# Laying the weight pieces of a gated last layer beside other chunks of an expert layer (attention, experts, SwiGLU on one core)

## The chip, the cores and the metric

The kernel runs on one core of one Trainium2 chip. A core has TensorE (PE in the rows; its weight loads are PEld), VectorE (DVE), ScalarE (ACT), GpSimd (POOL) and SyncE (SP, which here only issues DMA transfers). Each engine takes its own instructions in the order of the program and waits on semaphores for the others. The metric is the device time of one execution in microseconds (us), the median of the runs.

## The reference

Three layers follow each other, all in float32, on 4 x 576 = 2304 tokens of width 512:

```
attn = softmax(scale * q k^T + mask) v          # 8 heads of 64; 4 local (32 keys), 4 strided (every 32nd)
x    = attn, heads side by side                 # 2304 x 512
e    = argmax(x @ w_gate)                       # one of 8 experts per token
x    = p_e * sigmoid(x @ w_output_gate)_e * (relu(x @ w1[e]) @ w2[e])      # 512 -> 1024 -> 512
xn   = x / sqrt(mean(x*x) + 1e-6) * rms_g
g, v = xn @ w_gate2, xn @ w_val                 # 512 -> 1536, twice
out  = (g * sigmoid(g) * v) @ w_out             # 1536 -> 512
```

## The kernel before, in words

**Precision.** Each float32 operand of a matmul is split into a rounded part (names that end in `hi` or `h`) and the rest (`lo`, `l`), and each product is made of three matmuls: hi x hi, hi x lo, lo x hi.

**Stages.** Attention and routing take the first 130 us. Then come the 8 experts, sorted by their number of tokens: the first, with room for 256 tokens, then the fullest with 384, then 352, 336, 320, 304, 288 and 272. Then comes the last layer in 6 blocks of 384 tokens.

**Experts.** An expert's hidden width of 1024 is cut into 8 chunks of 128, so there are 64 chunks, `ch` 0 to 63; chunks 0 to 7 belong to the first expert, 8 to 15 to the fullest. For a chunk, `up(ch)` makes 12 matmuls into `hps` (L752 to L754), ScalarE writes `hhi` (L757) and VectorE `hlo` (L758); `down(ch)` makes 12 matmuls into four banks `y` (L776 to L778). TensorE's order is up(1), down(0), up(2), down(1) and so on; before chunks 4 and 5 of an expert stand transposes (L721) of the next expert's tokens, which ScalarE and VectorE take out (`xhi` L738, `xlo` L739). A chunk's weights are one transfer of 512 KB (`raw`, L176, four buffers), asked for four chunks ahead and split two chunks ahead into `whi` (ScalarE, L184) and `wlo` (VectorE, L185), three buffers. A `raw` transfer waits until VectorE has split the chunk that had the buffer before. GpSimd gathers the next expert's tokens (`xg`, L194), for the fullest expert three tiles of up to 128 rows of 528 float32 values.

**Pieces of the last layer's first weights.** `w_gate2` and `w_val` come as 24 pieces of 512 KB (float32 words and, of each, the bits that the narrow type takes), two for each of the 12 chunks of the width 1536. `prep_gv` transfers a piece into `gvr` (L653, two buffers), and `narrow` makes `gvh` and `gvl` of it with seven instructions: ScalarE L100 (`n_ab`, reads `gvr`) and L109 (`gvh`), VectorE L102, L105, L106, L108 (on `n_a`) and L110 (`gvl`). L109 waits for L108, L110 for L109. The table `GVC` names the chunks beside which the pieces stand, in order. Only the first VectorE instruction is tied to a place (behind the `wlo` of two chunks on); where the others and the transfer stand in their engines' queues is decided by the scheduler, which goes by times of its own, and so the tables' effect is seen in the order of the built program alone.

**Last layer.** `up2(u)` makes 24 matmuls of 384 columns into two banks `g` (L928 to L930), then follow sg (ScalarE L933, VectorE L934 and L935), `ahi` (ScalarE L938) and `alo` (VectorE L939); `down2(u)` makes 9 matmuls of 512 columns (L952 to L954) behind `up2(u + 1)`. In the first block (u = 0 to 11) the 12 pieces of `w_out` (`wr`, L899) are narrowed as well, by the same `narrow`, into `woh` and `wol`, one for each u, needed by `down2(u)`. Pieces of `GVC` that have no place beside an expert come here too, at u = 0, 2, 4 and so on; they share the two buffers of `wr`. In each block the next block is normalised: sums of squares (ScalarE L665, VectorE L667), `ss` (TensorE L676), `f` (VectorE L678, L679, GpSimd L680, VectorE L681), `fb` (TensorE L688).

```python
            if ch in GVC:
                prep_gv(pr_p, GVC.index(ch), queue_behind(last_split))
...
            if u % 2 == 0 and GV1 + u // 2 < 2 * NFC2:
                prep_gv(wr_p, GV1 + u // 2, queue_behind(last_up))
```

Of the kernel before, what the change touches and what calls it, by code (L numbers as in the profile page):

```python
# [41 lines left out]
BLK = 384  # L42
NBLK = N // BLK
WARM = (1, 2, 4, 2, 2, 1, 1)
GVC = (1, 3, 5, 7, 9, 11, 13, 15, 17, 19, 21, 24, 26, 28, 31, 33, 36, 39, 41, 44, 47, 50, 53, 57)
GV1 = len(GVC)
PB0 = (44, 46, 49, 51, 55, 57, 59, 61)
NB = (1, 3, 4, 5, 7, 8, 9, 10)
# [65 lines left out]
def attention_moe_swiglu(ctx: ExitStack, tc, qkv, va_l, va_s, wgd, cst_p, cst_a, cst_o, w12, wgv, wo, rmsg, out):  # L114
# [521 lines left out]
    def queue_behind(to):  # L636

        return lambda ins: tc.add_manual_dep(
            ins, to.name, mybir.DependencyInfo(mybir.DependencyClass.NoSync, mybir.DependencyReason.DATA),
            reason="order of issue on one engine")  # L640
# [9 lines left out]
    def prep_gv(pool, i, order=None):  # L650
        i, s = divmod(i, 2)
        r = pool.tile([128, KD * 128, 2], U32, tag="wr", name="gvr", bufs=2)
        nc.sync.dma_start(out=r.rearrange("p n w -> p (n w)"), in_=wgv[i, s].bitcast(U32))  # L653
        narrow(nc, pool, r, gvh[i][:, s].rearrange("p k f -> p (k f)"), gvl[i][:, s].rearrange("p k f -> p (k f)"), order)
# [47 lines left out]
    with m1:  # L702
# [7 lines left out]
        def turn_x(r, ks=range(KD)):  # L710
            cap = CAPS[r]
            if r in xT:
                hi, lo = xT[r]
            else:
                hi = xt_p.tile([128, KD, CAP], F32R, tag="xhi", name="xhi")
                lo = xt_p.tile([128, KD, CAP], F32R, tag="xlo", name="xlo")
                xT[r] = (hi, lo)

            def turn(j, k, ps):
                o, n, g = xg_t[r, j]  # L720
                nc.tensor.transpose(out=ps[:, o:o + n], in_=g[0:n, 128 * k:128 * (k + 1)],  # L721
                                    identity=cs("ident", n)[:, 0:n])

            nj = -(-cap // 128)
            if r == 0:

                pss = [ps_y.tile([128, CAP], F32, tag=f"y{k}", name="xp0") for k in range(KD)]
                for j in range(nj):
                    for k in range(KD):
                        turn(j, k, pss[k])  # L730
            for k in ks:
                if r == 0:
                    ps = pss[k]
                else:
                    ps = ps_x.tile([128, CAP], F32, tag="xp", name="xp")
                    for j in range(nj):
                        turn(j, k, ps)
                nc.scalar.copy(out=hi[:, k, 0:cap], in_=ps[:, 0:cap])  # L738
                nc.vector.tensor_tensor(out=lo[:, k, 0:cap], in0=ps[:, 0:cap], in1=hi[:, k, 0:cap].bitcast(F32),  # L739
                                        op=ALU.subtract)  # L740
# [96 lines left out]
        for ch in range(NCH):  # L837
# [11 lines left out]
            if fc in (4, 5) and r + 1 < E:  # L849
                turn_x(r + 1, (0, 1) if fc == 4 else (2, 3))  # L850
            if ch in GVC:
                prep_gv(pr_p, GVC.index(ch), queue_behind(last_split))
            if ch == 4:
# [327 lines left out]
```

## Time and profile before

| | us |
|---|---|
| runs | 853.64, 852.37, 849.71; median 852.37 |
| the profiled execution | 846.85 |
| its span, first to last instruction | 844.9 |
| TensorE busy in it | 825.6 |
| VectorE, ScalarE, GpSimd busy | 487.0, 335.6, 78.2 |

The profile is of one execution, which is 5.5 us shorter than the median of the runs. TensorE's busy time holds each matmul's whole passage through the array; matmuls overlap, so the pace of a row of matmuls is the distance of their starts, not their duration.

### The profile page before, as it was taken

The numbers are of one execution on the slowest core, as the hardware profiler recorded it, in microseconds if no ns is written. First come the engines' busy times: TensorE is split into PE (matmuls) and PEld (weight loads), VectorE is DVE, ScalarE is ACT, GpSimd is POOL, SyncE is SP. The second block draws the span as 40 slices with busy tenths as digits, with TensorE's granted clock in tenths as the row PEclk, the third lists the DMA queues.
The fourth block names the chain that finished last, engine by engine and source line by source line (L and its number), as shares of the span: only waits on it lengthen the run. The fifth ranks groups of instructions, "written<-read, shape, count | busy, mean of one in ns | idle before, by whom it ended". The sixth has DMA issues, their size and how long they took to land.

```text
span 844.9 us, 13837 instructions
## 1 busy us (share of the span) xinstructions
PE 825.6 (98%) x5230; PEld 766.6 (91%) x5230; DVE 487.0 (58%) x1342; ACT 335.6 (40%) x699; POOL 78.2 (9%) x76
## 2 busy tenths in 40 slices
PE   9999997999999999999999999999999999999996
PEld 6998865899999999999999999999999999999995
DVE  3889986978877788868875252234225222422221
ACT  3777644755556556644433131122213111212111
POOL 0000002425321101000001000100000010001001
PEclk9999999999999999999999999999999999999998
DMA  8788217899897697534321010101011010001000
GB/s 331 275 292 294 64 38 250 277 260 218 261 242 217 229 281 247 180 121 138 94 93 38 1 38 1 38 1 38 1 38 38 1 38 1 2 0 38 1 1 38
DMA packets 41765, 100.39 MB, mean 119 GB/s; under 512 B 9440, under 2 KB 23136, under 8 KB 41696
## 3 DMA queue, kind: packets, MB, share of 16 engines
q1 hardware_dynamic: 37840, 89.45, 34.2%
q0 software_dynamic: 3856, 10.05, 3.4%
q8 instruction: 41, 0.67, 0.3%
q14 instruction: 28, 0.23, 0.1%
HBM read 84.73 MB, written 14.75 MB: 118 GB/s over the span
## 4 chain that ended last, share of the span: by engine, by line
PE 73%; issue 15%; DVE 6%; DMA 3%; ACT 1%; POOL 1%; POOLq 0%; SPq 0%
PE g L928 8%; PE g L929 8%; PE g L930 8%; PE hps L752 4%; PE hps L753 4%; PE hps L754 4%; PE y L777 4%; PE y L778 4%; PE y L776 4%; PE o L953 4%; PE o L954 4%; PE o L952 4%; PE ops L349 3%; PE tps L331 2%; PE s L304 2%
## 5 line engine op out<-in xcount | busy, mean ns | idle before, releaser
L934 DVE TENSOR_TENSOR sg<-sg,g 128x384 f32<-128x384 f32 x72 | 39.8, 553 | 150.5 <-ACT sg L933 150.3
L933 ACT ACTIVATE sg<-g 128x384 f32<-128x384 f32 x72 | 35.3, 490 | 176.1 <-PE g L930 175.9
L185 DVE TENSOR_TENSOR wlo<-raw,whi 128x1024 fp32r<-128x1024 f32 (+1 forms) x66 | 78.6, 1192 | 33.6 <-ACT whi L184 29.4
L928 PE MATMUL g<-xn1h,gvh 128*128 128x384 f32 x288 | 97.7, 339 | 0.0
L929 PE MATMUL g<-xn1l,gvh 128*128 128x384 f32 x288 | 97.3, 338 | 0.0
L930 PE MATMUL g<-xn1h,gvl 128*128 128x384 f32 x288 | 97.1, 337 | 0.0
L928 PE MATMUL g<-xn0h,gvh 128*128 128x384 f32 x288 | 96.8, 336 | 0.0
L929 PE MATMUL g<-xn0l,gvh 128*128 128x384 f32 x288 | 96.4, 335 | 0.0
L930 PE MATMUL g<-xn0h,gvl 128*128 128x384 f32 x288 | 96.3, 335 | 0.0
L938 ACT CAST ahi<-sg 128x384 fp32r<-128x384 f32 x72 | 36.8, 512 | 132.1 <-DVE sg L935 132.1
L953 PE MATMUL o<-wol,ahi 128*128 128x512 f32 x216 | 85.4, 396 | 0.0
L954 PE MATMUL o<-woh,alo 128*128 128x512 f32 x216 | 85.2, 394 | 0.0
L952 PE MATMUL o<-woh,ahi 128*128 128x512 f32 x216 | 85.2, 394 | 0.0
L184 ACT CAST whi<-raw 128x1024 fp32r<-128x1024 f32 (+1 forms) x66 | 67.6, 1024 | 43.2 <-PE y L777 39.2
L752 PE MATMUL hps<-xhi,whi 128*128 128x256 f32 (+7 forms) x256 | 80.6, 315 | 0.8 <-ACT xhi L738 0.6
L754 PE MATMUL hps<-xhi,wlo 128*128 128x256 f32 (+7 forms) x256 | 79.4, 310 | 1.4 <-DVE wlo L185 1.4
L777 PE MATMUL y<-hlo,whi 128*128 128x256 f32 (+7 forms) x256 | 78.2, 306 | 2.1 <-DVE hlo L758 2.1
L753 PE MATMUL hps<-xlo,whi 128*128 128x256 f32 (+7 forms) x256 | 78.9, 308 | 0.4 <-DVE xlo L739 0.4
L778 PE MATMUL y<-hhi,wlo 128*128 128x256 f32 (+7 forms) x256 | 78.1, 306 | 0.0
L776 PE MATMUL y<-hhi,whi 128*128 128x256 f32 (+7 forms) x256 | 77.8, 306 | 0.0
L323 ACT ACTIVATE p<-u,nm 96x128 f32<-96x128 f32 (+2 forms) x176 | 60.1, 389 | 41.6 <-DVE nm L314 41.4
L935 DVE TENSOR_TENSOR sg<-sg,g 128x384 f32<-128x384 f32 x72 | 39.9, 554 | 59.1 <-PE g L930 58.7
(176 smaller groups left out, 1658.6 us busy)
## 6 DMA issues: line engine op xcount, KB each, us to landing
raw<-in_w SPq DMA_DIRECT2D x62, 512.0 KB
gvr<-in_wgv SPq DMA_DIRECT2D x24, 512.0 KB
qk<-in_qkv SPq DMA_DIRECT2D x14, 864.0 KB
wr<-in_wo SPq DMA_DIRECT2D x12, 512.0 KB
va<-in_va_l SPq DMA_DIRECT2D x4, 972.0 KB
yb<-yt_dram SPq DMA_DIRECT2D x20, 192.0 KB
va<-in_va_s SPq DMA_DIRECT2D x3, 810.0 KB
x_dram<-xs SPq DMA_DIRECT2D x24, 96.0 KB
```

The source lines that it names most:

```text
L752: mm(out=ps, lhsT=wh[:, w], rhs=xh[:, k, 0:cap], start=(k == 0), stop=False)
L753: mm(out=ps, lhsT=wh[:, w], rhs=xl[:, k, 0:cap], start=False, stop=False)
L754: last = mm(out=ps, lhsT=wl[:, w], rhs=xh[:, k, 0:cap], start=False, stop=(k == KD - 1))
L776: mm(out=ps, lhsT=wh[:, w], rhs=hi, start=(fc == 0), stop=False)
L777: mm(out=ps, lhsT=wh[:, w], rhs=lo, start=False, stop=False)
L778: mm(out=ps, lhsT=wl[:, w], rhs=hi, start=False, stop=(fc == NFC1 - 1))
L928: mm(out=ps, lhsT=wh, rhs=xh[d], start=(d == 0), stop=False)
L929: mm(out=ps, lhsT=wh, rhs=xl[d], start=False, stop=False)
L930: last_mm = mm(out=ps, lhsT=wl, rhs=xh[d], start=False, stop=(d == KD - 1)).ins
L952: mm(out=po[j], lhsT=hi[:, s], rhs=woh[i], start=(i == 0), stop=False)
L953: mm(out=po[j], lhsT=hi[:, s], rhs=wol[i], start=False, stop=False)
L954: mm(out=po[j], lhsT=lo[:, s], rhs=woh[i], start=False, stop=(i == NFC2 - 1))
```

## The change

The table of places is replaced, and nothing else:

```diff
-GVC = (1, 3, 5, 7, 9, 11, 13, 15, 17, 19, 21, 24, 26, 28, 31, 33, 36, 39, 41, 44, 47, 50, 53, 57)
+GVC = (6, 8, 9, 11, 14, 15, 17, 19, 22, 23, 25, 27, 30, 32, 34, 35, 38, 40, 43, 47, 50, 54)
 GV1 = len(GVC)
```

Pieces beside the experts, first to last: 4, 4, 3, 4, 3, 3, 2, 1 before; 1, 5, 4, 3, 4, 3, 2, 0 now. The table has 22 places in place of 24, so the last two pieces (both of the last chunk of the width 1536, read first by `up2(11)`) go to the last layer's first block, to u = 0 and u = 2.

ScalarE, from the end of `up(1)` in the first expert on. `hhi` is a chunk's rectified hidden part (chunks 1, 2, 3 and so on), `whi` a chunk's split weights (chunks 3, 4, 5 and so on), `n_ab<-gvr` the first instruction of a piece. Before:

```order
L757 ACTIVATE hhi<-hps 128x256
L184 CAST whi<-raw 128x1024
L757 ACTIVATE hhi<-hps 128x256
L100 ACTIVATE n_ab<-gvr 128x512
L184 CAST whi<-raw 128x1024
L757 ACTIVATE hhi<-hps 128x256
L184 CAST whi<-raw 128x1024
L109 CAST gvh_2472<-n_a 128x512
L100 ACTIVATE n_ab<-gvr 128x512
```

The same place now:

```order
L757 ACTIVATE hhi<-hps 128x256
L184 CAST whi<-raw 128x1024
L757 ACTIVATE hhi<-hps 128x256
L184 CAST whi<-raw 128x1024
L100 ACTIVATE n_ab<-gvr 128x512
L757 ACTIVATE hhi<-hps 128x256
L184 CAST whi<-raw 128x1024
L757 ACTIVATE hhi<-hps 128x256
L184 CAST whi<-raw 128x1024
L738 CAST xhi<-xp 128x384 x2
```

The piece of chunk 6 begins on ScalarE almost where the piece of chunk 1 began, one instruction later: behind `whi` of chunk 4, ahead of `hhi` of chunk 3. The other pieces' instructions are gone from here.

SyncE, from the transfer of chunk 5's weights on (`raw` of chunks 5, 6, 7 and so on; `gvr` are pieces; L166 and L782 read an expert's number or offset into a register). The difference at this place, before with -, now with +:

```order
@@ -115,44 +115,50 @@
 L176 ISA
 L176 DMA raw<-in_w 128x1024
-L653 DMA gvr<-in_wgv 128x1024
-L176 ISA
-L176 DMA raw<-in_w 128x1024
-L653 DMA gvr<-in_wgv 128x1024
-L176 ISA
-L176 DMA raw<-in_w 128x1024
-L166 TENSOR_LOAD rank_i
-L166 ISA x2
```

and now:

```order
+L176 ISA
+L176 DMA raw<-in_w 128x1024
+L166 TENSOR_LOAD rank_i
+L166 ISA x2
+L653 DMA gvr<-in_wgv 128x1024
+L176 ISA
+L176 DMA raw<-in_w 128x1024
```

The row with the first `gvr` stood behind `raw` of chunk 5 and stands now behind `raw` of chunk 7 and a register read.

TensorE in the first block of the last layer, around the normalisation of the next block: `ss` is the sum over the width, `fb` the factor spread over the partitions. Before, from the second k-step of `up2(5)` to the first matmul of `up2(6)`, in parts:

```order
L928 MATMUL g_5959<-xn0h,gvh_2477 128x384
L676 MATMUL ss<-cst_p_sb,s 128x1 x3
L929 MATMUL g_5959<-xn0l,gvh_2477 128x384
...
L954 MATMUL o_5765<-woh_5628,alo 128x512
L688 MATMUL fb<-cst_p_sb,f 128x128 x3
L928 MATMUL g_6017<-xn0h,gvh_2478 128x384
```

Now, from the thirteenth matmul of `up2(6)` to the first of `down2(5)`:

```order
L928 MATMUL g_6030<-xn0h,gvh_2478 128x384
L676 MATMUL ss<-cst_p_sb,s 128x1 x3
L929 MATMUL g_6030<-xn0l,gvh_2478 128x384
...
L930 MATMUL g_6030<-xn0h,gvl_2490 128x384
L688 MATMUL fb<-cst_p_sb,f 128x128 x3
L952 MATMUL o_5746<-woh_5607,ahi 128x512
```

Both go one u later, and where 20 matmuls of `up2` and 9 of `down2` stood between `ss` and `fb`, 11 of `up2` stand now. On VectorE each of the two pieces stands as a whole ahead of a piece of `w_out`: the first behind `wol` of u = 1, the second behind `wol` of u = 3.

## Rows read from the trace of the kernel before

**Rows 1.** The page's busy times: us, share of the span, instructions.
```profile
PE 825.6 (98%) x5230; PEld 766.6 (91%) x5230; DVE 487.0 (58%) x1342; ACT 335.6 (40%) x699; POOL 78.2 (9%) x76
```
**Rows 2.** Busy time of each engine by stretch: stretch, length, busy, clock, DMA share, GB/s.
```profile
134.30:164.10 29.80, 25.57 (x193) 24.23 (x194) 24.07 (x43) 18.52 (x32) 7.62 (x7) 0.94 0.87 308
164.10:198.00 33.90, 33.90 (x207) 33.82 (x206) 28.63 (x44) 20.17 (x34) 15.39 (x14) 1.00 0.91 239
...
198.00:230.10 32.10, 32.10 (x205) 32.06 (x205) 26.59 (x40) 19.55 (x32) 12.48 (x11) 1.00 0.92 247
...
376.30:410.00 33.70, 33.37 (x183) 31.40 (x182) 27.00 (x49) 15.00 (x29) 1.26 (x1) 1.00 0.43 137
```
**Rows 3.** TensorE in order of time: start, duration, line, tiles.
```profile
143.06 0.28 PE L752 MATMUL hps<-xhi,whi 128*128 128x256 f32 x1
...
145.10 0.28 PE L752 MATMUL hps<-xhi,whi 128*128 128x256 f32 x1
...
164.09 0.33 PE L752 MATMUL hps<-xhi,whi 128*128 128x384 f32 x1
...
164.44 0.34 PE L754 MATMUL hps<-xhi,wlo 128*128 128x384 f32 x1
```
**Rows 4.** TensorE's waits in the first expert, in order of time: [idle <- releaser].
```profile
147.96 0.38 PE L777 MATMUL y<-hlo,whi 128*128 128x256 f32 x1 [1.10 <-DVE hlo L758]
...
150.43 0.39 PE L754 MATMUL hps<-xhi,wlo 128*128 128x256 f32 x1 [0.66 <-DVE wlo L185]
...
160.35 0.38 PE L777 MATMUL y<-hlo,whi 128*128 128x256 f32 x1 [1.04 <-DVE hlo L758]
```
**Rows 5.** ScalarE and VectorE behind those waits, in order of time.
```profile
147.15 0.67 ACT L100 ACTIVATE n_ab<-gvr 128x512 f32<-128x512 f32 x1 [2.82 <-DMA gvr<-in_wgv]
...
147.15 0.43 DVE L102 TENSOR_SCALAR n_a<-gvr 128x512 uint32<-128x512 uint32 x1 [1.91 <-DMA gvr<-in_wgv]
...
155.34 0.39 ACT L757 ACTIVATE hhi<-hps 128x256 fp32r<-128x256 f32 x1 [0.34 <-PE hps L754]
...
159.89 0.41 DVE L758 SCALAR_TENSOR_TENSOR hlo<-hps,hhi 128x256 fp32r<-128x256 f32 x1
```
**Rows 6.** Busy time in the stretch of the third wait, columns as rows 2.
```profile
155.00:163.00 8.00, 6.96 (x60) 6.64 (x59) 8.00 (x17) 4.86 (x10) 3.97 (x3) 1.00 0.80 265
```
**Rows 7.** Busy time of the instructions on `n_a` alone: VectorE, ScalarE, clock, DMA.
```profile
376.30:451.00 74.70, 38.21 (x60) 7.40 (x12) 1.00 0.33 107
```
**Rows 8.** SyncE's issues in the first expert, in order of time.
```profile
140.80 0.34 SPq L653 DMA_DIRECT2D gvr<-in_wgv  x1
142.47 0.33 SPq L176 DMA_DIRECT2D raw<-in_w  x1
...
145.27 5.46 SPq L176 DMA_DIRECT2D raw<-in_w  x2
```
**Rows 9.** Busy time and GB/s while these transfers ran, columns as rows 2.
```profile
145.90:149.30 3.40, 2.30 (x20) 2.09 (x19) 2.12 (x5) 1.89 (x3) 0.28 (x1) 1.00 0.96 360
```
**Rows 10.** VectorE and TensorE in the last layer's first block, in order of time.
```profile
388.63 0.69 DVE L110 TENSOR_TENSOR wol<-n_a,woh 128x512 fp32r<-128x512 f32 x1 [0.15 <-ACT woh L109]
...
392.99 0.69 DVE L110 TENSOR_TENSOR wol<-n_a,woh 128x512 fp32r<-128x512 f32 x1 [0.22 <-ACT woh L109]
...
397.32 0.39 PE L952 MATMUL o<-woh,ahi 128*128 128x512 f32 x1
...
406.87 0.83 PE L676 MATMUL ss<-cst_p_sb,s 128*128 128x1 f32 x6 [0.33 <-DVE s L667]
...
410.04 0.16 DVE L681 TENSOR_TENSOR f<-f,gd 128x3 f32<-128x3 f32 x1 [0.74 <-POOL f L680]
```
**Rows 11.** Busy time and granted clock around the end of routing, columns as rows 2.
```profile
130.00:134.00 4.00, 1.74 (x10) 0.84 (x8) 2.73 (x13) 1.16 (x4) 0.30 (x1) 1.00 0.80 224
134.00:138.00 4.00, 3.33 (x17) 3.13 (x18) 3.51 (x8) 2.66 (x7) 0.00 (x0) 0.70 0.82 263
138.00:139.00 1.00, 1.00 (x6) 1.00 (x6) 0.26 (x1) 0.25 (x1) 0.00 (x0) 0.50 1.01 389
```

## The prediction

> **What bounds the kernel now.** I read the page first: TensorE is busy for 825.6 of 844.9 us [rows 1], so only its idle time and its pace can move the end. The busy times by stretch then say where idle time is: beside the fullest and the third expert TensorE is busy for all of 33.90 and 32.10 us, and beside the first for 25.57 of 29.80, with VectorE at 24.07; the first block of the last layer misses 0.33 us of 33.70 [rows 2]. Moving work off VectorE can therefore gain in the first expert alone, and elsewhere the move can only lose.
>
> For the size I take TensorE's pace from starts: 18 matmuls of 256 columns in 145.10 - 143.06 = 2.04 us, 0.113 each, and 0.175 for 384 columns [rows 3]. Twelve matmuls of the first expert last 1.36 us, so a chunk's 24 take 2.72 us. Three waits break this pace: 1.10 us at 147.96, 0.66 at 150.43 and 1.04 at 160.35 [rows 4]. A wait costs more than its idle time: the matmul ahead of it counts as busy for 0.28 us where the pace is 0.113 (+0.17), and the first one behind it takes about 0.1 longer. So they cost 1.37 + 0.93 + 1.31 = 3.6 us, which bounds the gain. The first 6 us of the expert lie before any piece is asked for [rows 8] and do not change.
>
> What ends these waits: the first two go back to the first piece, which landed at 147.15. VectorE's first instruction of it, ahead of `hlo` of chunk 2, had kept VectorE idle for 1.91 us, and ScalarE's, ahead of the split of chunk 4, ScalarE for 2.82 us [rows 5]. The third is VectorE's own queue: `hhi` of chunk 5 was ready at 155.7, `hlo` began at 159.89 [rows 5], and between 155 and 163 VectorE was busy for 8.00 of 8.00 us [rows 6].
>
> **The change, part by part.**
>
> *A piece's cost.* In the last layer 12 pieces kept VectorE busy for 38.21 us, ScalarE's `gvh` half apart [rows 7]: 3.18 us of VectorE a piece.
>
> *First expert, third wait.* Less 3.18 us for one piece, VectorE's 8.00 us [rows 6] become 4.8, so `hlo` no longer comes late: 1.31 us gained. The one piece left has its VectorE part behind the split of chunk 8, at the expert's end.
>
> *First expert, first two waits.* They do not go, by the order: `n_ab<-gvr` still stands ahead of `hhi` of chunk 3 on ScalarE, and its transfer now stands behind three `raw` transfers, of which the third (chunk 7) was issued at 145.27, when the split of chunk 3 was done [rows 8]. Some 0.35 us for that issue and a register read lie ahead of the piece: I put it at 146.3. When it lands has two bounds. Before, it took 147.15 - 140.80 = 6.35 us [rows 5, 8], which would be 152.65. At the 360 GB/s that the queues gave here [rows 9], what is asked for from 142.47 on (three loads of 524 KB and the 811 KB of the gather, 2.38 MB) needs 6.6 us: 149.1 at the earliest. I take the middle, 150.9. Behind it come `n_ab` (0.6), `hhi` (0.4) and `hlo` (0.4, as in rows 5), so TensorE's second matmul of down(3) starts at 152.35.
>
> And TensorE? Without the first wait, up(3) begins at 145.10 as before, down(2) at 146.46, up(4) at 147.83, and at 149.2 it stands still until 152.35, with nothing else in its queue that could go first. Before, up(4) went on from 150.43 [rows 4] and the same matmul of down(3) came 12 matmuls later, at 151.8. So one wait of 3.1 us takes the place of two, and the point is reached 0.55 us later. With the third wait gone, the next expert begins 1.31 - 0.55 = 0.76 us sooner than at 164.09 [rows 3]. With the two bounds of the landing this is 2.5 sooner to 1.0 later.
>
> *The fullest expert and the others.* Five pieces in place of four: 28.63 + 3.18 = 31.8 us of VectorE beside 33.90 of TensorE; the third expert's fourth piece gives 26.59 + 3.18 = 29.8 of 32.10 [rows 2]. Weights are split two chunks ahead and `hlo` has a chunk of slack (24 x 0.175 = 4.2 us). The tightest place is two pieces in a row, chunks 8 and 9: with each chunk's splitting (8.00 us less a piece in rows 6, 4.8 us for nearly two chunks and their transposes, so 2.4 each) 6.4 + 4.8 = 11.2 us beside 8.4, 2.8 us late, inside the 4.2. I take 0, and 2.8 as the upper bound. The experts from the fourth on have as many pieces as an expert before them had without a wait.
>
> *Last layer, first block.* Two more pieces, 6.36 us of VectorE, where it is busy for 27.00 of 33.70 us [rows 2]: 33.4, with no room left. I walked the two queues in the new order, with the steps of rows 7 and 10. `wol` of u = 2, which began at 392.99 [rows 10], follows a whole other piece (3.18) and a cast on ScalarE with nothing else to do meanwhile (1.0): it begins at 397.2 and ends at 397.85. down2(2) starts at 397.32 [rows 10] and wants it 0.2 later: 0.35 us of waiting. `wol` of u = 4 is 6.4 us later in the same way and misses by about as much: 0.35. Third, `fb`: from `ss` at 406.87 to the end of `f` at 410.2 it takes 3.3 us [rows 10]. Before, 20 matmuls of up2 and 9 of down2 covered this; now 11 of up2 do, 11 x 0.175 = 1.9 us with 0.3 for `ss` itself: 1.15 us of waiting. Given back is the wait of `ss` for its sums (0.33 of idle time, 0.5 with what surrounds it). Sum: 0.35 + 0.35 + 1.15 - 0.5 = 1.35 us lost. Lower bound 0, if the `wol` come in time and `fb` is covered by a late `ss`; upper bound all of 6.36.
>
> *Sum.* -0.76 + 0 + 1.35 = +0.6 us. On the profiled execution's 846.85 that is 847.45. The median of the runs stands 5.5 us above it, and the change adds nothing that would scale, so I put the same 0.6 on the median: 853.0. By the bounds of the landing, and half of the last layer's range either way, this case reaches from 849.8 to 856.
>
> **The rivals.**
>
> *ScalarE isn't held.* If the piece lands before hhi of chunk 3 is due (by about 147.5, so that `hhi` is there at 149.0), all three waits go: 3.6 us. With the last layer's terms covered this gives 848.8. For it: two fewer transfers lie ahead, 1.05 MB of them. Against it: the issue itself comes at 146.3, and no load of this size was seen to land within 1.2 us.
>
> *The clock falls.* Between 130 and 134 TensorE was busy for 1.74 of 4.00 us, and afterwards its granted clock was 0.70 on the mean of 134 to 138 and 0.50, the 1.2 GHz level, from 138 to 139 [rows 11]: 0.3 x 4 + 0.5 x 1 = 1.7 us of full clock lost. The waits of 1.1 us left the clock at 1.00 [rows 9]; my wait of 3.1 us is in between. If the clock falls behind it as it did there, the time is 854.7. The Trainium skill (TensorE: Matmul & The Clock Gate, "HAM oscillation — how this bites in real kernels") says that idle gaps between matmuls close the clock gate; by that rule a wait in which TensorE does nothing would bring this 854.7, by the waits of rows 9 the clock holds and 853.0 stands.
>
> *Slower.* VectorE becomes the bound of the last layer's first block: each wait there makes the next one late, and the 6.36 us lie on the path in full. With the first expert's gain that is +5.6 us: 858.0. It decides from the point where VectorE's 6.7 us of idle time in 376 to 410 [rows 2] can't be used. For it: one engine's order of 12 pieces with a cast on ScalarE in the middle of each. Against it: behind u = 5 the deadlines of `wol` have some 5 us of slack before, and the pieces' load ends there.
>
> *It does nothing.* The waits of the first expert only change places and the last layer hides its two pieces: 852.4. It lies inside my own case and has no price of its own.
>
> **How the numbers follow.** A measurement of this kernel can't tell 0.5% (4.3 us) from no change. My case, with the last rival, has 0.50; ScalarE not held 0.17; the clock 0.17; VectorE the bound 0.08; and 0.08 is for what I have not seen, half of it on each side. The predicted time is 853.0. Its own range of 849.8 to 856 must reach 848.8 below to take in the first rival; the clock (854.7) with the landing's upper bound comes to 856.5 above. Left out are the slower rival and the unseen: 848.5 to 856.5. Faster by over 0.5% means under 848.1, which needs the first rival and something more: 0.05. Slower by over 0.5% means above 856.6: the slower rival and a little: 0.10. Within 0.5%: 0.85.
>
> **What would show it.** In the changed profile ScalarE's first `n_ab<-gvr` has the longest idle time of the first expert ahead of it, ended by the transfer, at 149 to 153, and TensorE waits for `hlo` once, some 3 us, in place of three times. There is no wait near the transposes. The fullest expert begins at 161.5 to 165, and in all experts behind it TensorE's busy share is 1. In the last layer's first block TensorE waits for `wol` of u = 2 or u = 4 and for `f` at `fb`, 1 to 3 us in all. The step most likely to be wrong is the landing of the one piece; then that VectorE's lateness in the last layer adds up and isn't caught up by u = 6; last that two pieces in a row hold up a split beside the fullest expert.

## The result, and the profile after

The changed kernel takes 861.71 us (median of 5 runs, 858.42 to 866.78) beside 852.37 (849.71 to 855.06) for the kernel before: a ratio of 1.0117, 95% interval 1.0089 to 1.0145. It is slower by 1.2%, and outside my range. Its profiled execution took 861.22 us with a span of 859.4; it has 14.5 us more than the span of before, which was of an execution shorter than all five of these runs (846.85).

The page's busy times of the changed kernel answer to [rows 1]: 7.7 us more of TensorE, with the same instructions.

```profile
PE 833.3 (97%) x5230; PEld 771.1 (90%) x5230; DVE 487.1 (57%) x1342; ACT 335.2 (39%) x699; POOL 75.1 (9%) x76
```

The busy times by stretch, columns as [rows 2]: the experts 0 (the first) to 4, and the last layer's first 33.9 us.

```profile
134.40:162.90 28.50, 25.59 (x193) 24.51 (x194) 17.29 (x30) 15.83 (x27) 8.18 (x8) 0.94 0.86 286
162.90:202.20 39.30, 37.04 (x206) 35.30 (x206) 29.25 (x45) 19.45 (x33) 14.10 (x14) 0.96 0.74 198
202.20:239.40 37.20, 34.20 (x206) 33.55 (x205) 26.35 (x41) 19.14 (x32) 10.27 (x11) 0.95 0.68 209
239.40:275.80 36.40, 33.84 (x206) 32.34 (x206) 26.53 (x40) 19.07 (x32) 9.20 (x9) 0.95 0.79 212
275.80:306.40 30.60, 30.60 (x206) 29.69 (x205) 25.73 (x41) 18.86 (x32) 2.98 (x3) 1.00 0.76 248
390.10:424.00 33.90, 33.90 (x185) 32.04 (x184) 28.44 (x50) 14.20 (x27) 0.00 (x0) 1.00 0.45 149
```

I measure an expert from its first matmul to the next expert's. The first now takes 28.48 us, 1.34 less. Experts 1 (the fullest), 2 and 3 take 39.31, 37.22 and 36.42 where they took 33.91, 32.12 and 31.90: 5.40 + 5.10 + 4.52 = 15.0 us lost. Experts 4 to 7 are as before within 0.05. The last layer's first block takes 0.67 more. The sum, -1.34 + 15.02 + 0.67 = 14.35, is the whole difference of the two spans but for 0.15. VectorE isn't the engine that ran out: it is busy for 29 of 39 us and for 26 of 36.

**Where experts 1 and 2 lose.** TensorE at the turn to the fullest expert, in order of time:

```profile
161.32 0.28 PE L754 MATMUL hps<-xhi,wlo 128*128 128x256 f32 x1
...
162.85 0.34 PE L752 MATMUL hps<-xhi,whi 128*128 128x384 f32 x1
...
165.80 0.38 PE L776 MATMUL y<-hhi,whi 128*128 128x256 f32 x1 [0.40 <-ACT hhi L757]
...
168.64 0.45 PE L752 MATMUL hps<-xhi,whi 128*128 128x384 f32 x1 [0.86 <-issue]
...
169.94 0.54 PE L754 MATMUL hps<-xhi,wlo 128*128 128x384 f32 x1 [0.68 <-DVE wlo L185]
```

And ScalarE in the same stretch, with its whole queue:

```profile
161.03 1.05 ACT L184 CAST whi<-raw 128x1024 fp32r<-128x1024 f32 x1 [1.83 <-PE y L778]
165.37 0.38 ACT L757 ACTIVATE hhi<-hps 128x256 fp32r<-128x256 f32 x1 [3.29 <-remote]
167.54 1.04 ACT L184 CAST whi<-raw 128x1024 fp32r<-128x1024 f32 x1 [1.79 <-PE y L778]
171.17 0.49 ACT L757 ACTIVATE hhi<-hps 128x384 fp32r<-128x384 f32 x1 [2.58 <-remote]
```

The 256-column `hhi` at 165.37 is that of chunk 7. By the program it waits for two things: the last matmul of up(7), which starts at 161.32 and ends at 161.60, and `hlo` of chunk 5, done by 156.2. ScalarE is free from 162.08. So it starts 3.8 us after the work that it waits for; the releaser is "remote", which means that the profile finds no instruction beside the signal. TensorE's next reader follows `hhi` in 0.05 us (165.75 to 165.80). No piece stands in this queue. The next `whi` (167.54, chunk 9) needs the last matmul of down(6) that reads `whi`, which ended at 162.89. TensorE then waits for work that waits for TensorE's own late signal.

Expert 2 the same, TensorE first, then ScalarE: `whi` of chunk 17 needs the last matmul of down(14) that reads `whi`, at 201.81.

```profile
201.81 0.34 PE L777 MATMUL y<-hlo,whi 128*128 128x384 f32 x1
...
205.98 0.34 PE L778 MATMUL y<-hhi,wlo 128*128 128x384 f32 x1
208.64 0.43 PE L752 MATMUL hps<-xhi,whi 128*128 128x352 f32 x1 [2.33 <-issue]
```

```profile
207.55 1.04 ACT L184 CAST whi<-raw 128x1024 fp32r<-128x1024 f32 x1 [6.62 <-PE y L778]
```

ScalarE stood idle for 6.62 us and got the signal 5.4 us after the matmul's end at 202.15.

The trace also records when each semaphore steps. For TensorE's it has no step from 198.17 to 207.52 (one, which `hhi` at 200.43 needed, is missing), then two, and six more from 209.71 to 209.94, 0.05 us apart; the eight matmuls that these belong to, in order, ended between 202.15 and 206.32. ScalarE starts 0.03 us behind the step that it needs (207.52, 207.55). So the signal itself is late, and several come in a bunch; of VectorE's and ScalarE's semaphores every step on record between 150 and 275 us is within 0.06 us of its instruction's end.

What runs in both stretches is GpSimd's row of indirect transfers: three gathers of tokens (`xg`) and, right behind, eight stores of token weights (`tg_dram`, L802, `put_weights`), beside experts 1, 2 and 3 alone, in both kernels. In the changed kernel's first run:

```profile
161.28 0.95 POOL L802 DMA_INDIRECT tg_dram<-tg,tr_dp  x1 [0.30 <-issue]
162.53 1.61 POOL L802 DMA_INDIRECT tg_dram<-tg,tr_dp  x1 [0.30 <-issue]
...
171.59 0.92 POOL L802 DMA_INDIRECT tg_dram<-tg,tr_dp  x1 [0.30 <-issue]
```

**Expert 3** is another matter: ScalarE's `n_ab<-gvr` of the piece of chunk 27 stands ahead of an `hhi`, and its transfer lands late: from its issue to this first read it takes 10.7 us, where the same kernel with its stores paced (experiment 1) takes 7.9 (233.95 to 241.87) in the same order, and TensorE doesn't wait there. SyncE's issues, ScalarE, TensorE:

```profile
245.62 0.41 SPq L784 DMA_DIRECT2D yt_dram<-ysb  x1
246.53 0.34 SPq L176 DMA_DIRECT2D raw<-in_w  x1
246.92 1.06 SPq L653 DMA_DIRECT2D gvr<-in_wgv  x1
```

```profile
257.59 0.66 ACT L100 ACTIVATE n_ab<-gvr 128x512 f32<-128x512 f32 x1 [3.89 <-DMA gvr<-in_wgv]
```

```profile
258.64 0.45 PE L776 MATMUL y<-hhi,whi 128*128 128x336 f32 x1 [2.46 <-ACT hhi L757]
```

**The clock** fell behind the waits of each of the three experts. Stretches of the changed kernel, columns as [rows 2]:

```profile
170.20:173.40 3.20, 3.20 (x11) 3.20 (x11) 1.41 (x3) 1.66 (x5) 2.00 (x2) 0.50 0.69 217
...
211.20:214.40 3.20, 3.20 (x13) 3.20 (x12) 3.13 (x6) 1.88 (x4) 0.00 (x0) 0.50 0.59 189
...
259.00:262.00 3.00, 2.91 (x11) 2.82 (x11) 2.58 (x5) 0.87 (x2) 0.00 (x0) 0.50 0.41 154
```

At 0.50, the 1.2 GHz level, 3.2 us hold 1.6 us of full-clock work, so about a third of each loss is clock (an estimate from these rows). The wait of 1.16 us in the first expert (below) left it at 1.00.

### The profile page after: what moved, and what is told of

Read it like the earlier page. It is cut to its first block, busy times and chain, and to the rows that moved or that the text cites. A ratio compares the mean times of both kernels' runs of the same rounds, so it can differ in the third digit from the quotient of the medians.

```text
span 859.4 us, 13855 instructions
## 1 busy us (share of the span) xinstructions
PE 833.3 (97%) x5230; PEld 771.1 (90%) x5230; DVE 487.1 (57%) x1342; ACT 335.2 (39%) x699; POOL 75.1 (9%) x76
## 4 chain that ended last, share of the span: by engine, by line
PE 70%; issue 15%; DVE 7%; DMA 4%; ACT 1%; POOL 1%; another core or an unknown queue 0%; SPq 0%; POOLq 0%; DVEq 0%; ACTq 0%
PE g L928 8%; PE g L929 8%; PE g L930 8%; PE y L778 4%; PE o L952 4%; PE o L953 4%; PE o L954 4%; PE y L777 4%; PE hps L752 4%; PE y L776 4%; PE hps L754 4%; PE hps L753 4%; PE ops L349 3%; PE tps L331 3%; PE s L304 3%
## 5 line engine op out<-in xcount | busy, mean ns | idle before, releaser
L776 PE MATMUL y<-hhi,whi 128*128 128x256 f32 (+7 forms) x256 | 79.9, 312 | 4.2 <-ACT hhi L757 4.0
L777 PE MATMUL y<-hlo,whi 128*128 128x256 f32 (+7 forms) x256 | 80.0, 313 | 0.2
```

Of the source, the lines that this page charges most:

```text
L776: mm(out=ps, lhsT=wh[:, w], rhs=hi, start=(fc == 0), stop=False)
L777: mm(out=ps, lhsT=wh[:, w], rhs=lo, start=False, stop=False)
```

## The experiments

They ran in four sets, each beside its own runs of the kernel before, whose median was 846.06, 850.43, 852.28 and 853.27. Only ratios within a set are compared. The first set ran on another chip than the second and third, and the fourth on a third one. All numbers stand in the table; "lost" is the length of experts 1, 2 and 3 in the profiled execution less 33.91, 32.12 and 31.90, and "distance" the mean distance of the starts of eight stores, first to third run (with 24 in one run, all three beside expert 1); losses under 0.02 stand as 0. The first two rows are those of the result.

| kernel | us | before | ratio (95%) | lost, us | distance, us |
|---|---|---|---|---|---|
| before, profiled execution | 846.85 | | | 0, 0, 0 | 1.49, 1.52, 1.55 |
| changed | 861.71 | 852.37 | 1.0117 (1.0089 to 1.0145) | 5.40, 5.10, 4.52 | 1.47, 1.28, 1.46 |
| changed, again | 859.04 | 850.43 | 1.011 (1.0079 to 1.0141) | 4.00, 4.39, 4.61 | 1.45, 1.28, 1.46 |
| changed, one a chunk | 845.46 | 846.06 | 1.000 (0.9988 to 1.0013) | 0, 0, 0 | 4.0 to 4.3 |
| the same, again | 846.84 | 850.43 | 0.9951 (0.9932 to 0.9971) | 0.19, 0, 0.23 | 4.0 to 4.2 |
| changed, two a chunk | 847.32 | 853.27 | 0.992 (0.9898 to 0.9942) | 1.02, 0, 0.08 | 1.92, 1.80, 1.71 |
| changed, runs two chunks later | 852.21 | 852.28 | 0.9996 (0.9974 to 1.0018) | 0.45, 2.91, 1.57 | 1.50, 1.31, 1.45 |
| changed, 24 in one run | 874.05 | 852.28 | 1.025 (1.0217 to 1.0284) | 25.99, 0, 0 | 1.35, 1.23, 1.23 |
| before, one a chunk | 845.57 | 846.06 | 0.9993 (0.9983 to 1.0003) | 0, 0, 0 | 4.0 to 4.3 |
| first expert's part alone | 844.88 | 846.06 | 0.9987 (0.9978 to 0.9996) | 0, 0, 0 | 1.60, 1.52, 1.38 |
| the same, again | 859.13 | 852.28 | 1.0079 (1.0061 to 1.0096) | 5.54, 3.19, 1.47 | 1.44, 1.42, 1.38 |
| the same, control | 863.17 | 853.27 | 1.0101 (1.0071 to 1.0131) | 5.64, 4.58, 2.24 | 1.48, 1.31, 1.38 |
| the rest of the experts alone | 848.88 | 846.06 | 1.0036 (1.0022 to 1.0051) | 0.15, 0, 4.02 | 1.64, 1.44, 1.59 |
| the same, again | 852.22 | 852.28 | 1.0002 (0.9978 to 1.0026) | 1.29, 0, 5.24 | 1.58, 1.46, 1.46 |
| without the piece of chunk 7 | 858.17 | 853.27 | 1.0039 (1.0017 to 1.006) | 1.20, 4.30, 4.88 | 1.40, 1.31, 1.31 |
| one piece, at chunk 7 | 859.30 | 853.27 | 1.0062 (1.004 to 1.0084) | 10.80, 4.04, 0 | 1.25, 1.31, 1.55 |
| last layer's part alone | 851.04 | 850.43 | 1.0003 (0.9991 to 1.0015) | 0.06, 3.94, 1.40 | 1.64, 1.31, 1.38 |
| first expert's part, one a chunk | 845.31 | 850.43 | 0.9939 (0.9917 to 0.996) | 0, 0, 0 | 4.0 to 4.3 |

**1. The stores paced.** The edit, in the changed kernel and in the one before, in parts; the order on TensorE, VectorE, ScalarE and SyncE stays the same row for row:

```diff
-            queue_behind(after)(put.ins)
+            tc.add_manual_dep(put.ins, after.name,
...
-            if fc == 1 and 1 <= r <= 3:
-                for t in range(8 * r - 8, 8 * r):
-                    put_weights(dp, t, last_get)
+            if 9 <= ch < 33:
+                put_weights(dp, ch - 9, last_split)
```

The first part makes a store wait for the instruction that it is put behind, here that chunk's split on VectorE.

> The changed kernel; only GpSimd's 24 stores of token weights (tg_dram, L802) are moved: before in three runs of eight, each run behind the gather of an expert's tokens (experts 1 to 3), now one a chunk, chunks 9 to 32, each waiting for that chunk's VectorE split. Theory A: the three long waits of the changed kernel (experts 1, 2 and 3, 5.4 + 5.1 + 4.5 us) come from these runs of indirect transfers, while which TensorE's signals reach the other engines up to 5 us late; paced, the waits go and the time is 861.7 - 15 = about 847, at most 851. Theory B: they come from the pieces themselves, five, four and three beside experts 1 to 3 in place of four, three and four, which make ScalarE or VectorE late; then GpSimd's order changes nothing: 858 to 864.

> The kernel before with the same pacing of the 24 stores. Theory A: the profiled execution of before had none of these waits (846.85), but the median of its runs is 5.5 us above it, about one such wait; paced, the median comes down to 847 to 849. Theory B: the runs of stores harm nothing: 850 to 854, as before.

Measured, GpSimd in the changed kernel paced, and its experts 1 to 3:

```profile
171.63 1.24 POOL L802 DMA_INDIRECT tg_dram<-tg,tr_dp  x1 [12.23 <-DVE wlo L185]
175.63 1.13 POOL L802 DMA_INDIRECT tg_dram<-tg,tr_dp  x1 [2.76 <-DVE wlo L185]
```

```profile
161.10:195.00 33.90, 33.90 (x207) 33.82 (x206) 28.24 (x43) 19.17 (x33) 9.18 (x9) 1.00 0.87 231
195.00:227.10 32.10, 32.10 (x206) 32.06 (x205) 26.37 (x41) 19.54 (x32) 11.19 (x11) 1.00 0.90 242
227.10:259.00 31.90, 31.90 (x206) 30.93 (x206) 26.28 (x40) 18.96 (x32) 11.07 (x11) 1.00 0.94 242
```

With all its five, four and three pieces in place TensorE doesn't stop once. Theory B, that the pieces themselves make an engine late, falls. That it was the pacing which removed the waits is not shown by this set: its runs of before were 6.3 us shorter than those of the result, and a kernel with the same pieces beside experts 1 and 2 and the stores in runs of eight ("the rest of the experts alone") lost 0.15 and 0 us there too. For the same reason the kernel before, paced (845.57 beside 846.06), says nothing for or against theory A. So the changed kernel had to be seen beside its paced form.

**2. The changed kernel beside its paced form**, both unedited otherwise.

> The changed kernel once more, unedited, beside the experiments: the kernel before took 846.1 us beside the first four of them, 6.3 less than in the runs of the result, so the changed kernel must be seen beside the same runs. Theory A, as far as it still stands (the waits in the experts 1 and 2 come from TensorE's late signals behind GpSimd's runs of indirect transfers, the one in expert 3 from a piece that lands late): all three again, 857 to 861, and the paced one beside it at 845.5. Theory C: the late signals belong to the first runs and not to the table; only expert 3's wait (4.0 us where the second part of the change was made alone), less 1.3 to 2 for the first expert and plus 0.7 in the last layer stay: 847.5 to 850.

> The changed kernel with one store of token weights a chunk, once more, so that both stand beside the same runs of before. Both theories: 845 to 846, ratio 0.999 to 1.001. By theory A the difference to the unedited one is 12 us or more, by theory C 3 to 4 us, which is expert 3's wait alone.

859.04 and 846.84: 12.2 us between them in one set, from the order of GpSimd's stores alone. Theory C falls. The late signals come back at the same instructions (`hhi` of chunk 7 at 164.53, idle 2.60 <-remote; up(7) ended at 161.5).

```profile
164.53 0.38 ACT L757 ACTIVATE hhi<-hps 128x256 fp32r<-128x256 f32 x1 [2.60 <-remote]
166.70 1.05 ACT L184 CAST whi<-raw 128x1024 fp32r<-128x1024 f32 x1 [1.79 <-PE y L778]
```

**3. The stores closer, later, in pairs.** In the changed kernel: `if ch == 9: for t in range(24)`; or `fc == 3` in place of `fc == 1`, each run behind `last_split`; or two a chunk for `1 <= fc <= 4`, each behind that chunk's split.

> The changed kernel with all 24 stores in one run behind the gather beside the fullest expert, in place of eight beside each of experts 1 to 3. If the waits follow the stores: those in expert 2 are gone and expert 1 has longer ones, over up to six chunks, 3 to 10 us more than now in it; expert 3's late piece keeps its wait (some 2.5 to 4 us) or loses part of it. If they hang on the pieces, expert 2 keeps its 4 to 5 us.

> The changed kernel with GpSimd's three runs of eight stores held back by two chunks (behind the split of an expert's fourth chunk in place of right behind the gather of tokens), still eight in a row. If it takes the gathers and stores in one row of eleven, the waits at the first two chunks of experts 1 and 2 go: 846 to 850. If a run of eight stores is enough by itself, the waits move two chunks on: about as the changed kernel, 1.008 to 1.012.

> The changed kernel with the 24 stores two a chunk, beside the second to fifth chunk of experts 1 to 3, each pair behind that chunk's VectorE split: about one in 2 us in place of one in 1.3 to 1.5. If the distance of the stores decides, the waits go, as with one a chunk: 845 to 848. If it takes a distance of a whole chunk, the waits stay in part: 850 to 856.

One run of 24: expert 1 loses 26.0 us, and experts 2 and 3 nothing. ScalarE there, and the three experts:

```profile
196.75 0.49 ACT L757 ACTIVATE hhi<-hps 128x384 fp32r<-128x384 f32 x1 [15.24 <-remote]
```

```profile
163.60:223.50 59.90, 41.00 (x206) 37.48 (x205) 29.44 (x45) 19.69 (x33) 25.05 (x26) 0.80 0.49 135
223.50:255.60 32.10, 32.10 (x205) 32.06 (x205) 26.37 (x41) 19.57 (x32) 2.94 (x3) 1.00 0.73 239
255.60:287.50 31.90, 31.90 (x206) 30.93 (x205) 26.19 (x40) 19.00 (x32) 2.79 (x3) 1.00 0.72 239
```

The waits follow the stores; I had expected 3 to 10 us more than the 4 to 5.4 of eight stores, and the loss grows faster than the number of stores. Expert 3's late piece is late by nothing once no stores run near it.

Two chunks later (852.21) the waits are smaller, not gone, and expert 4 loses 1.8 us too (32.43 for 30.60). But the edit did not leave eight stores alone: the next expert's three gathers now stand right behind them, so each row has eleven again, and whether eight by themselves are enough is not shown:

```profile
192.36 0.92 POOL L802 DMA_INDIRECT tg_dram<-tg,tr_dp  x1 [0.30 <-issue]
193.58 0.98 POOL L194 DMA_INDIRECT xg<-x_dram,rows_x  x1 [0.30 <-issue]
```

In pairs the waits are nearly gone (847.32). The two stores of a pair are as close as in the runs of eight, 1.2 to 1.5 us; what is new is the pause of 1.7 to 2.9 us between pairs, so this is no test of the distance alone. The 1.02 us of expert 1 are lost before the stores begin, behind three gathers in a row (158.04 to 161.63): ScalarE's `whi` waits there for the last matmul of down(5) that reads `whi`, which ended at 160.70. So gathers can do it too, to a smaller degree:

```profile
162.38 1.05 ACT L184 CAST whi<-raw 128x1024 fp32r<-128x1024 f32 x1 [2.55 <-PE hps L754]
```

**4. Which part of the table sets them off.** Tables with one part of the change each:

```diff
-GVC = (1, 3, 5, 7, 9, 11, 13, 15, 17, 19, 21, 24, 26, 28, 31, 33, 36, 39, 41, 44, 47, 50, 53, 57)
+GVC = (6, 9, 11, 13, 15, 17, 19, 21, 24, 26, 28, 31, 33, 35, 36, 39, 41, 43, 44, 47, 49, 50, 53, 57)
+GVC = (1, 3, 5, 7, 8, 9, 11, 14, 15, 17, 19, 22, 23, 25, 27, 30, 32, 34, 38, 40, 43, 47, 50, 54)
+GVC = (1, 3, 5, 7, 9, 11, 13, 15, 17, 19, 21, 24, 26, 28, 31, 33, 36, 39, 41, 44, 47, 50)
```

> The kernel before with only the first expert's part of the change: pieces at chunks 1, 3, 5 and 7 become one at chunk 6, the three others go beside the experts from the fifth on (chunks 35, 43, 49 among others); beside experts 1 to 3 the table is that of before, the last layer keeps none. The first expert should end about 1.3 us sooner. Theory A (the long waits hang on how the runs of stores meet the other transfers, not on the number of pieces): long waits in the experts 1 to 3 appear here too, since everything behind the first expert has shifted: 855 to 862. Theory B (five pieces beside the fullest expert and those behind it do it): no long waits, 850 to 852.

> The other part alone: the first expert keeps its pieces at 1, 3, 5 and 7, the fullest and those behind it have the places of the changed kernel (8, 9, 11, 14, 15, 17, 19, 22, 23 and so on), 24 in all, so the last layer keeps none. Theory B: the long waits of experts 1 to 3 come with these places: 860 to 866, as the changed kernel and 1.3 us for the first expert. Theory A with the shift of the first expert as what sets them off: 850 to 856.

> The kernel before with the last two entries of its table (53 and 57) taken out, so that these two pieces go to the last layer's first block, and nothing else: the prediction's third term by itself, put there at +1.35 us (0 to 6.4). By the changed kernel's trace the last layer is 0.7 us longer: 846.8. If VectorE became the bound of that block, 850 and above.

> The first expert's part alone (one piece, at chunk 6; experts 1 to 3 with the pieces of before), once more; which share of the 1.1% is its own. Beside runs in which TensorE's signals come late at all (before at 850 rather than 846): theory A1, the first expert's part alone sets the late signals off, since all that follows is shifted against the stores: ratio 1.004 to 1.010. Theory A2, they take the denser pieces beside experts 1 to 3: 0.997 to 1.000. Beside quiet runs (before at 846) both give 0.9987.

> The other part alone (first expert as before, the places of the changed kernel from chunk 8 on, none in the last layer), once more. Theory A2: nearly all of the loss is here, ratio 1.009 to 1.013. Theory A1: only the late piece of expert 3, 1.0036 as it was in the quiet runs.

Where signals come late at all, it is the first expert's part: 1.0079, against 1.0002 for the rest of the experts and 1.0003 for the last layer's. So A1, and A2 falls. (A ratio of 1 does not say that a kernel loses nothing: before at 852.28 is itself 6.2 us above the first set.) Beside before at 846 the same program gained 0.13% and lost nothing: whether signals come late depends on something outside the program too, and chip and time are not parted here. The changed kernel itself has no run in that set; the first expert's part (-1.2 us) and the rest (+2.8) add up to an estimate of +1.6, without the last layer's term.

One sign goes with it. In the trace of before and in the four of the first set, every step of the semaphores of TensorE, VectorE and ScalarE between 150 and 275 us is on record, and TensorE's are on time. In the other thirteen traces 6 to 17% of VectorE's and ScalarE's steps are missing, around the indirect transfers, and TensorE's come late: 3, 3 and 9 of them (over 0.06 us behind any matmul's end) in those with one or two stores a chunk, 11 to 29 in those with runs.

The rest alone loses 4.0 and 5.2 us in expert 3 at the late piece (ScalarE there, in the first of the two):

```profile
246.26 0.66 ACT L100 ACTIVATE n_ab<-gvr 128x512 f32<-128x512 f32 x1 [4.42 <-DMA gvr<-in_wgv]
```

**5. Why the first expert's part.** Tables as that part, with the piece of 7 alone taken out of the first expert, or with the one piece at 7.

> The kernel before with only the piece of chunk 7 taken from the first expert (it goes to chunk 49): three pieces beside the first expert, so it ends about as before, but VectorE has a piece less where the first run of stores goes out. Theory A1a (VectorE's work keeps the stores apart): as the control, slower than before by 4 to 7 us where the control is. Theory A1b (the earlier start of all that follows): as before, within 2 us.

> The first expert's part alone with the one piece at chunk 7 in place of 6: the experts from 1 on start about as early as in the control, but VectorE has the piece to do where the first run of stores goes out. Theory A1a: faster than the control by 3 to 6 us, at about the time of before or 1 us under it. Theory A1b: as the control, within 2 us.

> Control, unedited from the earlier runs: the first expert's part alone with its piece at chunk 6. It had a ratio of 0.9987 beside quiet runs and 1.0079 beside runs with late signals. If this one is again near 1.008 the two tables beside it tell the theories apart; if it is near 0.999 they don't.

Inconclusive. Taking away piece 7 alone costs 0.39%, and leaving the piece at 7 is 3.9 us better than the control in the median, both as A1a has it. But the intervals of the latter two overlap, and of their profiled executions the one with the piece at 7 is the longer (spans of 858.7 and 856.6). By A1a it should also be no slower than before, and is, by 0.62%, with 10.8 us lost in expert 1. Nor is A1b put to the test: without the piece of 7 the first expert took 28.65 us, as little as with one piece at chunk 6 (28.56 in the mean), and in the control 29.06.

**6. The first expert's part and the paced stores together.**

> The first expert's part alone (one piece, at chunk 6) together with the paced stores. If the two gains are of different places they add up: 0.9987 x 0.9993, that is 844.4; if pacing is worth nothing where no transfer is late, as without it: 844.9.

845.31, 0.6% faster than before, and 1.6% than the changed kernel of that set: the shortest of its set.

## Why the prediction was wrong

**The step that failed** is "The fullest expert and the others": I took 0, with 2.8 us as the upper bound, and 15.0 were lost there. I looked for VectorE's lateness, and that stayed inside its slack as I had worked out (the paced kernel has the two pieces in a row at chunks 8 and 9 and not one wait). What I left out stood in the kernel before: GpSimd's runs of indirect transfers beside just these experts, behind which TensorE's signals come late. The trace of before could not show these waits, since in it every signal is on time. A hint lay in my own sum. The median of before stood 5.5 us above its profiled execution, and I wrote that the change adds nothing that would scale. That the runs of before hold some of these waits is borne out by the last-layer part alone: it has the order of before in experts 1 to 3, and lost 3.94 and 1.40 us in its profiled execution; and beside before at 850.4, the first expert's part with paced stores took 845.3. No trace of before itself with such waits was kept.

The second thing missed in that step is expert 3's `n_ab` ahead of an `hhi`: the same order that I had priced in the first expert, 2.46 us of waiting and the clock behind it. The order alone does not cost this (paced, it costs nothing); it takes the slow landing beside the stores as well. I had not walked ScalarE's queue where the pieces moved by one or two chunks.

**First expert, third wait:** right. VectorE is busy for 4.43 us in 155 to 163 (I had 4.8; 8.00 in [rows 6]) and TensorE for all 8.00:

```profile
155.00:163.00 8.00, 8.00 (x70) 8.00 (x69) 4.43 (x8) 3.62 (x6) 4.37 (x5) 1.00 0.74 235
```

**First expert, first two waits:** the mechanism was right, the size off. ScalarE is held, but the piece's read began at 149.51 where I had 150.9, inside my bounds of 149.1 and 152.65; so one wait of 1.16 us in place of 3.1, and for `hhi`, not `hlo`. That the landing came near is in part luck. I had read the order wrong, and so had the section on the change: the piece's transfer stands behind `raw` of chunk 6 and a register read, ahead of `raw` of chunk 7 (142.10, 144.34, 144.82). So it was issued at 144.34 where I had 146.3, and took 5.2 us to the read where I had 4.6. TensorE also waited 0.52 us for a gather ahead of the transposes, where I had written that no wait would be. The expert is 1.34 us shorter (I had 0.76). Over the profiled executions of all kernels it took 28.8 to 29.8 us with the four pieces (mean of five 29.16) and 27.4 to 30.8 with the one at chunk 6 (mean of eleven 28.56), a gain of 0.6, which is near my figure. SyncE, ScalarE, then TensorE:

```profile
142.10 0.33 SPq L176 DMA_DIRECT2D raw<-in_w  x1
144.34 0.01 SPq L653 DMA_DIRECT2D gvr<-in_wgv  x1
144.82 0.34 SPq L176 DMA_DIRECT2D raw<-in_w  x1
```

```profile
149.51 0.66 ACT L100 ACTIVATE n_ab<-gvr 128x512 f32<-128x512 f32 x1 [3.46 <-DMA gvr<-in_wgv]
```

```profile
150.49 0.38 PE L776 MATMUL y<-hhi,whi 128*128 128x256 f32 x1 [1.16 <-ACT hhi L757]
153.21 0.66 PE L721 MATMUL xp<-cst_p_sb,xg 128*128 128x128 f32 x4 [0.52 <-DMA xg<-x_dram,rows_x]
```

**Last layer:** +0.67 for +1.35, in the places that I named: the wait of `ss` is gone, one for `woh` of u = 4 and one for `fb` came. The part alone measured 1.0003 (0.9991 to 1.0015), that is -0.8 to +1.3 us. Over the profiled executions of all kernels the last layer's first block took 74.5 to 75.0 us without the two pieces (mean of ten 74.73) and 75.5 to 76.0 with them (mean of eight 75.75): 1.0 more, nearer to my figure. TensorE in the changed kernel:

```profile
424.87 0.97 PE L952 MATMUL o<-woh,ahi 128*128 128x512 f32 x3 [0.37 <-ACT woh L109]
...
431.79 0.91 PE L688 MATMUL fb<-cst_p_sb,f 128*128 128x128 f32 x6 [0.24 <-DVE f L681]
```

**The clock** held in the first expert, so that rival did not come in its place; it came three times behind the waits that I had not seen. The rule that I cited from the Trainium skill (TensorE: Matmul & The Clock Gate, "HAM oscillation — how this bites in real kernels"), that idle gaps close the gate, the trace bears out there: 0.50 behind idle times of 2.33 and 2.46 us, 1.00 behind 1.16. At the turn to the fullest expert it was 0.50 behind three shorter ones, 0.40, 0.86 and 0.68 us. And in one other execution the rival did come: with one store a chunk, in the second set, the first expert's wait was 1.67 us, the clock fell, and the expert took 30.8 us, the longest of all:

```profile
151.00 0.38 PE L776 MATMUL y<-hhi,whi 128*128 128x256 f32 x1 [1.67 <-ACT hhi L757]
152.20:155.40 3.20, 3.20 (x17) 3.02 (x16) 2.10 (x3) 1.80 (x3) 0.00 (x0) 0.50 0.95 335
```

**The range.** My case's 849.8 to 856 is not what its bounds add up to: the landing's 1.8 us either way and half of the last layer's room (0.7 down, 2.5 up) give 850.5 to 857.3. The measured 861.7 lies above both.

**Left open.** Why TensorE's signals are late while the indirect transfers run, what differs between the sets, and why the first expert's part brings it on more than the table of before. That closer stores go with more loss is seen in the table: with runs of eight, experts 1 and 2 lost 2.9 us or more at distances of 1.25 to 1.48 us and 1.3 or less at 1.40 to 1.64. But these overlap, expert 3's run at 1.38 us lost nothing once and 2.24 another time, and cause and effect may be turned round. No run parted these.

## What to carry to other kernels

When a wait's releaser is "remote" or a matmul that ended microseconds ago, look for what else is in flight, not at the engines' queues: here 24 small indirect stores, off every engine's path, cost 12 us where signals came late, and giving each a place of its own behind a later instruction removed it (two a chunk did nearly as well). A median well above the profiled execution says that something may come in some executions that this profile doesn't show; find it before pricing a change that shifts the phase. And where a table moves pieces, walk the in-order queue at every place where a transfer's first reader now stands ahead of the path's own work.

## What was not expected of the hardware

Signals of TensorE reached ScalarE 3.8 and 5.4 us after the matmul's end in the changed kernel, and one wait lasted 15.24 us with 24 indirect stores in a row; ScalarE's signal to TensorE took 0.05 us in the same stretch. The late steps then came in bunches, 0.05 us apart. The Trainium skill (Perfetto Trace Analysis, "Tensor Engine Instruction (MATMUL, LD_WEIGHTS)") says that a matmul's end in a profile is estimated, and that its signal goes out only when PSUM has acknowledged the writes and must then spread; it gives no time for either, and the runs here don't tell which of the two was slow.
